# Products of ones on the tensor engine between the counts of a routing search, a fifth raw buffer, and a step that waits longer

## The chip, the cores and the metric

The kernel runs on one core of a Trainium2 chip, as one launch. The time is the device time of that core in microseconds (us), the median of three runs. TensorE (PE) multiplies, VectorE (DVE) and ScalarE (ACT) do elementwise work and move results out of PSUM, the matmul's output memory; GpSimd (POOL) issues gathers, and SyncE (SP) issues the other transfers.

## The reference

Three layers follow each other on 2304 tokens of 512 numbers. The second decides which tokens go where, and the change stands there.

```python
# 1. attention: 4 x 8 heads, 576 positions, window of 128, bias by distance
x = attention(q, k, v)                      # 2304 x 512
# 2. capacity-limited mixture: 8 experts, 288 tokens each
logits = x @ w_gate                         # 2304 x 8
for idx in argsort(-logits.flatten()):      # greedy, best logit first
    tok, e = idx // 8, idx % 8
    if assigned[tok] < 0 and counts[e] < 288:
        assigned[tok] = e; counts[e] += 1
for e in range(8):
    out[assigned == e] = relu(x[assigned == e] @ w1[e]) @ w2[e]   # 512 -> 1024 -> 512
# 3. weighted mixture: 4 experts on every token
for e in range(4):
    out2 += p[:, e:e+1] * (relu(out @ m2w1[e]) @ m2w2[e])
```

## The kernel before

Each matmul of 32-bit numbers is done as three: operands are split into an upper and a lower part (`wh`, `wl`; `xh`, `xl`), and `mm3` adds upper x upper, upper x lower and lower x upper (lines 791 to 793 are `hid_mm`'s and `mm3`'s three products).

Attention runs until about 157 us. Then come the eight groups of the second layer, one for each expert that becomes full, in the order in which they do. Group g begins with a search (`routing_steps`): six rounds, each of a `count` (PE: how many tokens wish each expert above each of n thresholds; two rounds with 18 products, line 559, four with 9, line 562), `enough` (DVE, tiles `odd` and `sat`), `any` (PE, tile `ns`) and `narrow` (DVE, tiles `pen`, `th`, `ge`). It closes with `who` (DVE, `r`), `many` (PE, `c`), `which` (DVE, `mk`), `totals` (PE, `tot`), `left` (DVE), `before` (PE, `pf`), `placed`, `tables` and `at` (DVE, `ob`), `numbers` (PE, `ls`, 18 products), `whole` (DVE, `idx`) and `gather` (POOL, `xg`). The next group's search starts with `wish` and `codes` (DVE, from `logits` to `oh`). A step depends on the one before, so PE and DVE take turns in it.

Once the rows are gathered, PE turns them (`rows`, tile `tp`), makes the 32 hidden steps `hid` (tile `hp_a`) and the 32 output steps `y` of the group, and then the first part of the third layer on these rows (`hp_f`, `po_f`). Each product of `hid` and `y` needs a piece of the expert's weights: 16 pieces for each group, loaded by SP into one of `NRAW` raw buffers (`raw_a`), copied to the upper part by ACT (`up`, `wh_a`) and subtracted by DVE (`low`, `wl_a`). Before them stand 12 pieces of the third layer's first expert (`raw_b`, `wl_b`). From about 625 us on PE does the rest of the third layer (`hp_b`, `po`).

The order of all steps from the search on is laid out beforehand by `arranged`: a list scheduler with a planned time for each step, which on each engine takes the open step of the lowest rank (search 1, weight pieces and `hid`/`y` 3). A step of rank 3 stands back if a step of lower rank opens within 0.4 of its planned time. Each engine then executes its steps in that order and waits by semaphores.

PSUM tiles come from pools; `ps_y` has two buffers:

```python
ps_y = ctx.enter_context(tc.tile_pool(name="ps_y", bufs=2, space=PSUM))
```

Of the kernel before, what the change touches and what calls it, by code (L numbers as in the profile page):

```python
# [9 lines left out]
F32 = mybir.dt.float32  # L10
# [9 lines left out]
P = 128  # L20
# [5 lines left out]
def fused_kernel(ctx: ExitStack, tc: tile.TileContext, q, k, v, w_gate, w1, w2, probs, m2w1, m2w2, out, dbg=None):  # L26
# [13 lines left out]
    NK = DM // P  # L40
    XC = DM + E2
    CB = 96
    NRAW = 4
    NB = CAP // CB
    HALF = F // 2
    KW = math.lcm(SEQ, P)
# [22 lines left out]
    def bc(ap, shape):  # L69
        return ap.broadcast_to(shape)  # L70
# [751 lines left out]
    def routing_steps(g):  # L822
        d = grp[g]
        prev = ("placed", g - 1) if g > 0 else None
        if g > 0:
            def wish():
                best_tiles(g)
                wishes(g, 0, NTL)
                if g < E - 1:
                    jl = rsm.tile([E, E], F32, tag="jl", name=f"jl_{g}")  # L830
                    V.tensor_tensor_reduce(jl, rem[:E, :], ident[:E, :E], 1.0, 0.0, ALU.mult, ALU.add, best["left"])
            step(("wish", g), DVE_, 3.0 if g < E - 1 else 1.4, wish, [("left", g - 1), ("at", 0, 1) if g == 1 else None], 1)
            step(("codes", g), DVE_, 0.5 if g < E - 1 else 0.1, lambda: wish_codes(g, 0, NTL), [("wish", g), prev], 1)
        else:
            def wish0():
                jl = rsm.tile([E, E], F32, tag="jl", name="jl_0")
                V.tensor_tensor_reduce(jl, rem[:E, :], ident[:E, :E], 1.0, 0.0, ALU.mult, ALU.add, best["left"])
            step(("codes", 0), DVE_, 0.1, wish0, [], 1)
        last = ("codes", g)
        if g < E - 1:  # L840
            for r in range(len(ROUNDS)):
                wide = ROUNDS[r][1] == 64
                now = {}

                def bind(i, g=g, r=r, now=now):
                    def run():
                        if not now:
                            now["f"] = ops_round(g, r)
                        now["f"][i]()
                    return run  # L850
                nx = r + 1 < len(ROUNDS)
                step(("count", g, r), PE_, 0.7 if wide else 0.45, bind(0), [last, ("keep", g - 2) if g > 1 and r == 0 else None], 1)
                step(("enough", g, r), DVE_, 0.28 if wide else 0.45, bind(1), [("count", g, r)], 1)
                step(("any", g, r), PE_, 0.2, bind(2), [("enough", g, r)], 1)
                step(("narrow", g, r), DVE_, (0.6 + (1.6 if ROUNDS[r + 1][1] == 64 else 0.95)) if nx else 0.5, bind(3), [("any", g, r)], 1)
                last = ("narrow", g, r)
        who, how_many, which, expert, totals, left_over, before, placed, tables, at_place, numbers, whole, gather = (
            (lambda i: lambda *a: closers(g)[i](*a))(i) for i in range(13)
        )
        if g < E - 1:  # L860
            step(("who", g), DVE_, 1.4, who, [last], 1)
            step(("many", g), PE_, 0.2, how_many, [("who", g)], 1)
            last = ("many", g)
        step(("which", g), DVE_, 0.95, which, [last] + ([prev, ("keep", g - 2)] if g == E - 1 else []), 1)
        step(("expert", g), SP_, 1.3, expert, [("which", g)], 1)
        step(("totals", g), PE_, 0.25, totals, [("which", g)], 1)
        step(("left", g), DVE_, 0.8, left_over, [("totals", g)], 1)
        step(("before", g), PE_, 0.3, before, [("left", g)], 1)
        step(("placed", g), DVE_, 0.55, placed, [("before", g)], 1)
        step(("tables", g), DVE_, 1.0, tables, [("placed", g)], 2 if g else 0)  # L870
        half = NTL // 2
        step(("at", g, 0), DVE_, 0.95, lambda: at_place(0, half), [("tables", g)], 2 if g else 0)
        step(("at", g, 1), DVE_, 0.95, lambda: at_place(half, NTL), [("at", g, 0)], 2 if g else 0)
        step(("numbers", g), PE_, 0.95, numbers, [("at", g, 1)], 1)
        step(("whole", g), DVE_, 0.2, whole, [("numbers", g)], 1)
        step(("gather", g), POOL_, 3.1, gather, [("whole", g), ("rows", g - 1, NK - 1) if g > 0 else None], 1)
# [8 lines left out]

    LAND = 4.5
    npieces = 0

    def pieces(n, job_of, known, free, names):
        nonlocal npieces  # L890
# [239 lines left out]
    def arranged():  # L1130

        order, ends, free, opened = [], {}, {}, {}
        waits = {n: len(t[2]) for n, t in tasks.items()}
        after = {n: [] for n in tasks}
        for n, t in tasks.items():
            for o, _ in t[2]:
                after[o].append(n)
        number = {n: i for i, n in enumerate(tasks)}

        def open_(n):  # L1140
            eng, _, needs, _, _ = tasks[n]
            at = 0.0
            for o, us in needs:
                lag = us if us is not None else (0.0 if tasks[o][0] == eng else 0.25)
                at = max(at, ends[o] + lag)
            opened.setdefault(eng, {})[n] = at

        for n, w in waits.items():
            if w == 0:
                open_(n)  # L1150
        while any(opened.values()):
            found = None
            for eng, names in opened.items():
                if not names:
                    continue
                now = max(free.get(eng, 0.0), min(names.values()))
                can = [n for n, at in names.items() if at <= now]

                def rank_of(n):
                    return 0.5 if eng == DVE_ and tasks[n][3] == 3 and now - names[n] > 1.5 and ("gather", 0) in ends else tasks[n][3]  # L1160
                n = min(can, key=lambda n: (rank_of(n), number[n]))
                us, rank = tasks[n][1], rank_of(n)

                soon = [o for o, at in names.items() if at < now + 0.4 * us and tasks[o][3] < min(rank, 2 if eng == "PE" else 3)]
                if rank >= 3 and soon:
                    n = min(soon, key=lambda o: names[o])
                start = max(now, names[n])
                if found is None or start < found[0]:
                    found = (start, n)
            start, n = found  # L1170
            eng, us, *_ = tasks[n]
            del opened[eng][n]
            free[eng] = ends[n] = start + us
            order.append((start, len(order), n))
            for o in after[n]:
                waits[o] -= 1
                if waits[o] == 0:
                    open_(o)
        assert len(order) == len(tasks)
        return sorted(order), ends  # L1180

    planned, ends = arranged()
# [87 lines left out]
```

## Time and profile before

| | us |
|---|---|
| median of three runs (1283.14 to 1286.18) | 1283.77 |
| profiled execution | 1285.34 |
| its span, first to last instruction | 1283.6 |
| PE busy in the span | 1227.5 |
| DVE busy | 635.5 |
| ACT busy | 404.7 |
| POOL busy | 216.7 |

The profile is of one execution. PE's busy time counts each product from its start to its modelled end, and products overlap, so starts of neighbours give their rate. PEclk is the granted clock of TensorE as a share of 2.4 GHz; the two levels that occur are 1.0 and 0.5 (1.2 GHz). In a timeline row, what stands in brackets is the engine's idle time before the row and what ended it.

### The profile page before, as it was taken

The numbers are of one execution on the slowest core, as the hardware profiler recorded it, in microseconds if no ns is written. First come the engines' busy times: TensorE is split into PE (matmuls) and PEld (weight loads), VectorE is DVE, ScalarE is ACT, GpSimd is POOL, SyncE is SP. The second block draws the span as 40 slices with busy tenths as digits, with TensorE's granted clock in tenths as the row PEclk, the third lists the DMA queues.
The fourth block names the chain that finished last, engine by engine and source line by source line (L and its number), as shares of the span: only waits on it lengthen the run. The fifth ranks groups of instructions, "written<-read, shape, count | busy, mean of one in ns | idle before, by whom it ended". The sixth has DMA issues, their size and how long they took to land.

```text
span 1283.6 us, 21264 instructions
## 1 busy us (share of the span) xinstructions
PE 1227.5 (96%) x8209; PEld 1110.7 (87%) x8209; DVE 635.5 (50%) x1828; ACT 404.7 (32%) x1041; POOL 216.7 (17%) x264
## 2 busy tenths in 40 slices
PE   7999828999999999999999999999999999999998
PEld 6998727888889899999988899899999998888896
DVE  6999888898768674443122233222222222222222
ACT  8998733333233343443211111111111111111110
POOL 8877501010000000000000111101101100100112
PEclk9999957899999999999999999999999999999999
DMA  9653144454444244564850011001000100000111
GB/s 182 149 142 76 51 132 135 157 107 121 117 147 136 78 161 110 169 132 111 313 203 1 23 44 33 33 1 34 25 9 17 33 17 17 17 1 1 41 42 65
DMA packets 125012, 108.58 MB, mean 85 GB/s; under 512 B 76272, under 2 KB 91632, under 8 KB 124912
## 3 DMA queue, kind: packets, MB, share of 16 engines
q1 hardware_dynamic: 121936, 97.76, 27.9%
q0 software_dynamic: 2976, 9.48, 2.2%
q8 instruction: 64, 1.05, 0.3%
q14 instruction: 36, 0.29, 0.1%
HBM read 83.53 MB, written 23.68 MB: 84 GB/s over the span
## 4 chain that ended last, share of the span: by engine, by line
PE 71%; DVE 9%; issue 5%; POOL 1%; DMA 1%; ACT 0%; POOLq 0%; SPq 0%; DVEq 0%
PE hp_b L791 8%; PE hp_b L793 8%; PE hp_b L792 8%; PE po L791 7%; PE po L793 7%; PE po L792 7%; PE hp_a L791 3%; PE hp_a L792 2%; PE hp_a L793 2%; PE po_f L791 2%; PE hp_f L791 2%; PE hp_f L793 2%; PE hp_f L792 2%; PE po_f L792 2%; PE po_f L793 2%
## 5 line engine op out<-in xcount | busy, mean ns | idle before, releaser
L800 ACT ACTIVATE hh_b<-hp_b 128x384 fp32r<-128x384 f32 x156 | 76.7, 492 | 535.8 <-PE hp_b L793 535.8
L803 DVE SCALAR_TENSOR_TENSOR hl_b<-hp_b,hh_b 128x384 fp32r<-128x384 f32 x156 | 87.0, 557 | 264.0 <-ACT hh_b L800 264.0
L793 PE MATMUL hp_b<-yTh,wl_b 128*128 128x384 f32 x624 | 209.5, 336 | 0.0
L791 PE MATMUL hp_b<-yTh,wh_b 128*128 128x384 f32 x624 | 209.5, 336 | 0.0
L792 PE MATMUL hp_b<-yTl,wh_b 128*128 128x384 f32 x624 | 209.4, 336 | 0.0
L1210 DVE SCALAR_TENSOR_TENSOR acc<-po,pp,acc 128x512 f32<-128x512 f32 x126 | 94.6, 751 | 219.0 <-PE po L793 219.0
L791 PE MATMUL po<-wh_b,hh_b 128*128 128x512 f32 x468 | 184.8, 395 | 0.0
L793 PE MATMUL po<-wh_b,hl_b 128*128 128x512 f32 x468 | 184.7, 395 | 0.0
L792 PE MATMUL po<-wl_b,hh_b 128*128 128x512 f32 x468 | 184.6, 395 | 0.0
L760 POOL TENSOR_TENSOR wl_b<-raw_b,wh_b 128x512 fp32r<-128x512 f32 x44 | 56.0, 1292 | 536.0 <-ACT wh_b L755 439.8
L791 PEld LDWEIGHTS hp_b<-yTh,wh_b 128*128 128x128 f32 x624 | 117.2, 188 | 1.8
L792 PEld LDWEIGHTS hp_b<-yTl,wh_b 128*128 128x128 f32 x624 | 117.2, 188 | 1.7
L793 PEld LDWEIGHTS hp_b<-yTh,wl_b 128*128 128x128 f32 x624 | 117.2, 188 | 0.0
L793 PEld LDWEIGHTS po<-wh_b,hl_b 128*128 128x128 f32 x468 | 87.7, 187 | 21.4
L792 PEld LDWEIGHTS po<-wl_b,hh_b 128*128 128x128 f32 x468 | 87.7, 187 | 19.5
L791 PEld LDWEIGHTS po<-wh_b,hh_b 128*128 128x128 f32 x468 | 87.7, 187 | 19.4
L760 DVE TENSOR_TENSOR wl_a<-raw_a,wh_a 128x512 fp32r<-128x512 f32 x128 | 84.0, 683 | 2.9 <-ACT wh_a L755 1.9
L721 POOL DMA_INDIRECT xg<-x_dram,idx x24 | 24.4, 1018 | 360.2 <-PE po_f L793 100.4
L791 PE MATMUL hp_a<-xh,wh_a 128*128 128x288 f32 x256 | 80.7, 315 | 0.0
L755 ACT CAST wh_a<-raw_a 128x512 fp32r<-128x512 f32 x128 | 73.6, 618 | 21.7 <-DMA raw_a<-in_moe_w_dram 21.6
L791 PE MATMUL y<-hh_a,wh_a 128*128 128x288 f32 x256 | 78.8, 308 | 0.0
L793 PE MATMUL y<-hh_a,wl_a 128*128 128x288 f32 x256 | 76.8, 300 | 1.7 <-DVE wl_a L760 1.7
(219 smaller groups left out, 2506.7 us busy)
## 6 DMA issues: line engine op xcount, KB each, us to landing
raw_a<-in_moe_w_dram SPq DMA_DIRECT2D x128, 256.0 KB, 3.2
raw_b<-in_moe_w_dram SPq DMA_DIRECT2D x64, 256.0 KB, 2.7
x_dram<-x SPq DMA_DIRECT2D x18, 258.0 KB, 2.6
y_dram<-yh SPq DMA_DIRECT2D x8, 576.0 KB, 3.1
y_dram<-yl SPq DMA_DIRECT2D x8, 576.0 KB, 4.6
yTh<-y_dram SPq DMA_DIRECT2D x6, 768.0 KB, 9.1
yTl<-y_dram SPq DMA_DIRECT2D x6, 768.0 KB, 10.5
acc<-part_dram SPq DMA_DIRECT2D x6, 768.0 KB, 11.3
```

Of the source, the lines that this page charges most:

```text
L721: G.indirect_dma_start(out=xg[:, j, :], out_offset=None, in_=x_dram[:, :], in_offset=bass.IndirectOffsetOnAxis(ap=d["idx"][:, j : j + 1], ...
L755: S.copy(res[n][0][0][:, a, b], raw)
L760: eng.tensor_tensor(lo[:, a, b], raw, hi[:, a, b].bitcast(F32), ALU.subtract)
L791: T.matmul(o, ah, bh, start=first, stop=False)
L792: T.matmul(o, ah, bl, start=False, stop=False)
L793: T.matmul(o, al, bh, start=False, stop=last)
L800: S.activation(h[0][:, f, :n], hp[:, :n], AF.Relu)
L803: V.scalar_tensor_tensor(h[1][:, f, :n], hp[:, :n], 0.0, h[0][:, f, :n].bitcast(F32), ALU.max, ALU.subtract)
L1210: V.scalar_tensor_tensor(accs[ch][:, i, :], po, pe, accs[ch][:, i, :], ALU.mult, ALU.add)
```

## The change

A new step `warm` multiplies a 128 x 128 matrix of ones by 256 columns of ones, into a tile of `ps_y` that nobody reads. 500 of them are offered to the planner on PE with a planned time of 0.115 us and rank 9, behind every other step; they stand back if a step of rank below 3 opens within 0.115 us. When the planner takes the first hidden step of group 0, those left over are dropped. `NRAW` becomes 5. The `wish` of group 1 waits for `whole` of group 0 in place of the last `at`. Until the first gather is planned, a weight piece stands back for a step that opens within 0.8 of its time.

```diff
-    NRAW = 4
+    NRAW = 5
...
-            step(("wish", g), DVE_, 3.0 if g < E - 1 else 1.4, wish, [("left", g - 1), ("at", 0, 1) if g == 1 else None], 1)
+            step(("wish", g), DVE_, 3.0 if g < E - 1 else 1.4, wish, [("left", g - 1), ("whole", 0) if g == 1 else None], 1)
...
+    def warm():
+        o = ps_y.tile([P, 512], F32, tag="y", name="warm")
+        T.matmul(o[:, :256], ones_bf, bc(ones_bf[:, None, :], [P, 2, P]), start=True, stop=True)
+
+    for i in range(500):
+        step(("warm", i), PE_, 0.115, warm, [("codes", 0)], 9)
...
-                soon = [o for o, at in names.items() if at < now + 0.4 * us and tasks[o][3] < min(rank, 2 if eng == "PE" else 3)]
+                near = 1.0 if rank == 9 else 0.4 if ("gather", 0) in ends else 0.8
+                soon = [o for o, at in names.items() if at < now + near * us and tasks[o][3] < min(rank, 2 if eng == "PE" and rank < 9 else 3)]
...
+            if n == ("hid", 0, 0, 0, 0):
+                for o in [o for o in opened[PE_] if o[0] == "warm"]:
+                    del opened[PE_][o]
...
-        assert len(order) == len(tasks)
+        assert all(n in ends or n[0] == "warm" for n in tasks)
```

PE, between the last two products of the first count and the product `ns` of the first round, as it stands before:

```order
L559 MATMUL cnt_0_3822<-ge_106,oh 8x64
L559 LDWEIGHTS oh
L559 MATMUL cnt_0_3822<-ge_106,oh 8x64
L578 LDWEIGHTS ones_bf
L578 MATMUL ns_0_3848<-sat_0_3821,ones_bf 128x64 [waits DVE_49]
L559 LDWEIGHTS oh
```

The same place now, from the last product of the count on; in brackets is the engine whose semaphore an instruction waits for:

```order
L559 MATMUL cnt_0_3822<-ge_106,oh 8x64
L893 LDWEIGHTS ones_bf
L893 MATMUL warm<-ones_bf 128x256
L893 LDWEIGHTS ones_bf
L893 MATMUL warm<-ones_bf 128x256
L893 LDWEIGHTS ones_bf
L893 MATMUL warm<-ones_bf 128x256 [waits PE_49]
L893 LDWEIGHTS ones_bf
L893 MATMUL warm<-ones_bf 128x256 [waits PE_49]
L893 LDWEIGHTS ones_bf
L893 MATMUL warm<-ones_bf 128x256 [waits PE_49]
L893 LDWEIGHTS ones_bf
```

Six `warm` stand between the count and `ns`; from the third on each waits for PE's own semaphore at the value that the `warm` two before it sets when it ends. Of all 304 that the planner placed, 302 wait so. They stand in runs of 6 (behind `cnt`), 23 (behind `ns`), 6, 17, then three times 8 and 17, then 8, 20 (ahead of `c`), 12 (ahead of `tot`), 11 (ahead of `pf`) and 34 (ahead of `ls`), which makes 212; behind `ls`, in the second group's search, 41, 6, 23, 6 and 12 ahead of the first `tp`; and 4 ahead of the first hidden product. The first `tp` stands behind the second group's second round; before, it stood behind the third.

DVE, behind `tables` of group 0 (`ob` is the last `at`), before:

```order
L694 TENSOR_TENSOR one_4097<-A_4090 128x54
L696 TENSOR_TENSOR R_4099<-one_4097,cp 128x108 [waits DVE_49]
L700 TENSOR_TENSOR ob_4101<-iotaB,bb_4095 128x864 x2
L117 TENSOR_TENSOR logits<-logits,capv 128x144
L118 TENSOR_REDUCE m_4106<-logits 128x18 [waits DVE_49]
```

and now:

```order
L694 TENSOR_TENSOR one_4467<-A_4460 128x54
L696 TENSOR_TENSOR R_4469<-one_4467,cp 128x108 [waits DVE_49]
L700 TENSOR_TENSOR ob_4471<-iotaB,bb_4465 128x864 x2
L716 TENSOR_REDUCE idx_4561<-ls_4532 96x3 [waits PE_49]
L117 TENSOR_TENSOR logits<-logits,capv 128x144
```

The `idx` that the gather waits for stands ahead of the second group's `wish` (which begins with `logits`); before, it stood behind it. On PE the order of counts, closing products, hidden and output products is otherwise the one that the planner's new times give; the second group's 16 weight pieces `wl_a` all stand on DVE ahead of that group's closing step `which`, where before the last three stood behind it.

## Rows read from the trace of the kernel before

**Rows 1.** Page: busy us by engine; granted clock in 40 slices, tenths.

```profile
PE 1227.5 (96%) x8209; PEld 1110.7 (87%) x8209; DVE 635.5 (50%) x1828; ACT 404.7 (32%) x1041; POOL 216.7 (17%) x264
...
PEclk9999957899999999999999999999999999999999
```

**Rows 2.** Windows: stretch, length, busy PE PEld DVE ACT POOL, clock, DMA, GB/s.

```profile
160.40:204.00 43.60, 14.26 (x151) 11.38 (x150) 38.26 (x123) 13.55 (x23) 4.45 (x3) 0.50 0.48 153
204.00:208.20 4.20, 4.20 (x19) 3.89 (x18) 2.76 (x11) 1.95 (x5) 0.00 (x0) 0.50 0.30 72
224.00:230.00 6.00, 3.11 (x31) 2.06 (x29) 5.62 (x24) 0.73 (x2) 0.00 (x0) 0.89 0.14 45
230.00:235.50 5.50, 5.50 (x27) 5.22 (x27) 4.22 (x9) 0.81 (x2) 0.00 (x0) 0.50 0.29 94
235.50:1240.00 1004.50, 1000.52 (x5998) 909.21 (x5996) 416.71 (x966) 237.29 (x508) 84.66 (x74) 1.00 0.26 77
```

**Rows 3.** Timeline of PE in the search: start, length, count, idle before.

```profile
157.17 0.63 PE L559 MATMUL cnt<-ge,oh 128*8 128x64 bf16 x16 [0.61 <-DVE lh L467]
158.78 0.22 PE L559 MATMUL cnt<-ge,oh 128*8 128x64 bf16 x2 [0.97 <-DVE oh L133]
159.36 0.18 PE L578 MATMUL ns<-sat,ones_bf 8*128 8x64 bf16 x1 [0.36 <-DVE sat L570]
161.18 1.30 PE L559 MATMUL cnt<-ge,oh 128*8 128x64 bf16 x18 [1.64 <-DVE ge L108]
...
169.65 0.80 PE L562 MATMUL cnt<-ge,oh 128*64 128x64 bf16 x9 [1.45 <-DVE ge L108]
171.11 0.20 PE L578 MATMUL ns<-sat,ones_bf 8*128 8x32 bf16 x1 [0.66 <-DVE sat L574]
...
187.40 1.85 PE L708 MATMUL ls<-R,ob 128*96 128x6 bf16 x18 [4.07 <-DVE ob L700]
...
201.10 1.70 PE L944 MATMUL tp<-ident,xg 96*128 96x96 f32 x9
...
203.98 0.59 PE L791 MATMUL hp_a<-xh,wh_a 128*128 128x288 f32 x1
204.37 0.44 PE L792 MATMUL hp_a<-xl,wh_a 128*128 128x288 f32 x1
204.61 0.44 PE L793 MATMUL hp_a<-xh,wl_a 128*128 128x288 f32 x1
```

**Rows 4.** Timeline of PE behind the first hidden product.

```profile
208.45 0.29 PE L793 MATMUL hp_a<-xh,wl_a 128*128 128x288 f32 x1
208.58 0.29 PE L791 MATMUL hp_a<-xh,wh_a 128*128 128x288 f32 x1
...
226.07 0.40 PE L793 MATMUL y<-hh_a,wl_a 128*128 128x288 f32 x1 [1.26 <-DVE wl_a L760]
227.64 0.69 PE L559 MATMUL cnt<-ge,oh 128*8 128x64 bf16 x18 [1.17 <-DVE oh L133]
...
229.24 0.61 PE L793 MATMUL y<-hh_a,wl_a 128*128 128x288 f32 x1 [0.46 <-DVE wl_a L760]
...
237.28 0.93 PE L708 MATMUL ls<-R,ob 128*96 128x6 bf16 x18
...
240.47 0.47 PE L562 MATMUL cnt<-ge,oh 128*64 128x64 bf16 x9
```

**Rows 5.** By tile: products' ns, least, median and most, from start to end.

```profile
L653 PE MATMUL tot<-ones_bf,mk x8: 231/231/291, 182.2 to 482.3; 128*36 128x128 bf16 x8
L791 PE MATMUL y<-hh_a,wh_a x45: 288/295/402, 236.0 to 300.0; 128*128 128x288 f32 x45
```

**Rows 6.** Timelines of DVE and POOL in the search: `sat`, `idx`, first gather.

```profile
159.04 0.27 DVE L570 TENSOR_SCALAR sat<-cnt,left 8x64 bf16<-8x64 f32 x1 [0.32 <-PE cnt L559]
...
191.22 0.15 DVE L716 TENSOR_REDUCE idx<-ls 96x3 int32<-96x6 f32 x1
...
191.67 1.17 POOL L721 DMA_INDIRECT xg<-x_dram,idx  x1 [37.96 <-DVE bm L131]
```

## Prediction

> **What bounds the kernel now.** I read the clock line and the TensorE line of the page first, then busy times by stretch, then the timelines of TensorE and VectorE from the first count on. TensorE has work in 96% of the span, and there is one long dip in the granted clock [rows 1]. The stretches [rows 2] say where. From 235.5 us to 1240 us TensorE is busy for 1000.5 of 1004.5 us at the full clock (2.4 GHz), so whatever starts that stream later ends the kernel later by as much. From 160.4 to 204 us it is busy for 14.3 of 43.6 us, at half clock (1.2 GHz): the first expert is being searched for, and products of 64 columns alternate with VectorE steps [rows 3]. The search ends for TensorE when the first expert's rows are turned (201.10 us) and the first hidden product starts (203.98 us). Behind it the clock stays at half until 208.2, and between 230 and 235.5 it is at half again, after three waits in the output products of 1.26, 1.17 and 0.46 us [rows 2, 4].
>
> **What the change puts on TensorE.** 304 products `warm` stand there before the first hidden product: 212 up to the products `ls` that number the rows (6, 23, 6, 17, then 8 and 17 in turn, 8, 20, 12, 11 and 34), 88 from there to the first `tp` (41, 6, 23, 6, 12) and 4 behind the last `tp`. The plan gives each 0.115 us. A stream without waits would come near that: 288 columns start every 0.13 us at full clock and every 0.24 us at half clock [rows 3, 4], so 256 columns every 0.12 us or 0.21 us.
>
> But 302 of the 304 wait for TensorE's own semaphore. `ps_y` has two buffers, so each `warm` waits until the one two before it has ended. The trace has no row in which TensorE waits for a product just issued; I build the price from two others. How long one takes from start to end: 0.231 us for 128 columns, 0.295 us for 288 [rows 5], so about 0.28 us for 256. How long a hand-over takes: the first count ends at 158.78 + 0.22 = 159.00 and `sat` starts at 159.04; `sat` ends at 159.31 and `ns` starts at 159.36 [rows 3, 6]; so 0.05 us. Two `warm` then take 0.28 + 0.05 = 0.33 us, each 0.165 us; as the first two of a run don't wait, I take 0.16 us on the mean. Bounds: 0.12 us if the wait never holds, 0.23 us if all ran at half clock (0.40 us from start to end, from the 0.44 us of 288 columns in [rows 3], plus 0.05, for two).
>
> At 0.16 us a run of `warm` is longer than the VectorE step beside which it stands, everywhere. Between `ns` and the next count VectorE now keeps TensorE idle for 1.64 us (wide round) and 1.45 us (narrow) [rows 3]; 23 and 17 `warm` take 3.7 and 2.7 us. Between a count and `ns` it is 0.36 and 0.66 us; 6 and 8 take 0.9 and 1.2 us. Ahead of `ls` it is 4.07 us; 34 take 5.5 us. The engine executes in order, so the count behind a run waits for it. TensorE's own stream then sets the length of the search.
>
> **The sum up to the first hidden product.** First count at 157.17, to 158.86 as now: 1.7 us. 300 `warm` x 0.16 = 48.0 us. At full clock three wide counts take 0.7 us each, four narrow ones 0.33 us each (0.47 us less the drain of the last), `ls` 0.9 us [rows 4]: 4.3 us. Twelve single products, 0.1 us each: 1.2 us. Together 55.2 us, so the first `tp` stands at 212.4 us against 201.10. From there 12 `tp` at half of now's 0.19 us, one count and 4 `warm` take 2.0 us (now 2.9 us): first hidden product at 214.4 us against 203.98, **10.4 us later**.
>
> **What comes back.** If the clock is at full when the hidden products start, the 4.2 us at half clock in 204.0 to 208.2 shrink by half: 2.1 us. With full clock in 230 to 235.5 too: 2.75 us. The three waits (2.9 us) I leave as they are. Weight pieces `wl_a` are nearer done when the hidden products start, and the new order has all 16 done before the second expert's closing steps; but its count rounds are one further behind and their products now stand between the hidden ones, so waits for `wl_a` turn into waits for `ge`, `r`, `mk` and `oh`. Bounds: 0 to all 2.9 us.
>
> Sum: 10.4 - 2.1 - 2.75 = **+5.6 us**. The profiled execution took 1285.34 us (span 1283.6 and 1.7 us around it), so it would take 1290.9 us; that run lies 1.6 us above the median of the runs shown, 1283.77, so the median becomes **1289.4 us**.
>
> **The parts I cost at nothing.** (a) `wish` of expert 1 behind `idx`. Now `ls` ends at 189.25, and `idx` waits behind that step until 191.22 [rows 3, 6]: 1.9 us for the gather. With the sum above the gather starts near 197.1 and has landed by 206.5 (9.43 us at most, 191.67 to 201.10 [rows 3, 6]), 6 us before TensorE gets to `tp`. Cover: 88 `warm`. Without it this part is worth those 1.9 us. (b) The wider look-ahead (0.8 of a step) before the first gather: VectorE takes one piece instead of two between `ge` and `odd`, which would be worth up to one piece; the 8 `warm` cover it. (c) The fifth raw buffer: loads run earlier, but in the search no piece is what TensorE waits for, and from 235.5 us on TensorE waits for 4.0 us in all.
>
> **A rule against my price.** The Trainium skill, "TensorE: Matmul & The Clock Gate", section "Back-to-back issue gap", gives about 109 ns from one such product to the next at full clock. The rows of 288 columns agree within 10 ns (133 against 122 ns), but none of them waits for its own engine. By it the sum would be that of the first rival.
>
> **Rivals.**
> 1. *The wait doesn't hold* (13%): 0.12 us each. 300 x 0.04 = 12 us less, of which VectorE takes back about 1 us ahead of `ls` and before `tp`: `tp` near 201.4, hidden products near 203.4, 0.6 us earlier than now. With 2.1 + 2.75 us back: 5.4 us faster, 1278.4 us. It decides below 0.14 us, where the search is 6 us shorter than in my sum. For it: the plan's own figure. Against it: the semaphore wait stands in the program.
> 2. *The clock falls among the products* (11%). Each pair leaves a pause, and the idle time around the first counts could drop the clock as it does now (half from 160.4 on [rows 2]). In a part at half clock a `warm` costs 0.07 us more; half of the 300 is 10 us, and the 2.1 us may not come back: near 1300 us. The same page of the Trainium skill ("A second HAM failure mode: psum-queue depth-cycling") reports a clock that swings where products cycle through PSUM banks with short pauses; no stretch of this trace shows such cycling. Against it: at half clock the same products stand nearly end to end, and the hidden products, end to end, brought the clock back at 208.2.
> 3. *The delay is taken up later* (14%). While TensorE is kept, VectorE gets ahead; then the three waits (2.9 us) go, and some of the 4.0 us after 235.5: 5.6 - 2.9 - 2 = +1 us, 1284.5 us, no difference that can be told. Against it: VectorE is in order, its pieces stand between steps that wait for TensorE.
> 4. *No effect* (2%): runs shorter than the steps beside them; 1284 us.
>
> **Chances and range.** About 0.3% (3.9 us) is what a measurement of this kernel tells from no change: 1279.9 and 1287.6. My case has 60%. Within it, 0.15 to 0.18 us for each is -3 to +6 us, and the waits give up to 2.9 us: 1283.5 to 1295.5 us. Some 8 of the 60 end below 1287.6. Slower: 52 + 11 = 63%. Same: 8 + 14 + 2 + 1 = 25%. Faster: 12%. The range leaves out the lower part of rival 1 and the upper part of rival 2: 1279 to 1298.
>
> **What the profile will show.** Right: `warm` starts in pairs, about 0.11 and 0.22 us apart in turn; 304 of them cover 48 us; every count of the search starts right behind a `warm` with no idle time whose releaser is VectorE; VectorE idles instead, waiting for `cnt` and `ns`; `ls` near 195.7, first `tp` near 212, first hidden product near 214, at full clock from its first row; no half clock around 230 to 245. Wrong: `warm` 0.12 us apart (rival 1), PEclk of 0.5 between 160 and 214 (rival 2), or a hidden product 10 us late but TensorE without idle time until the gap is made up (rival 3). The sum hangs most on the time of a pair: 0.01 us there is 1.5 us of it.

## The result, and the profile after

The changed kernel took 1297.35 us (median of four runs, 1295.53 to 1300.48) beside 1283.80 us for the kernel before on the same chip: 13.55 us slower, ratio 1.0104 with a 95% interval of 1.0092 to 1.0116. The forecast was 1289.4 us, 5.6 us slower. The direction and the range hold; the size is off by 8 us. The profiled execution is the slowest of the four (1300.48 us, span 1298.8), so its rows stand 3.1 us above the median.

The page of the changed kernel answers [rows 1]: TensorE's busy time and its clock in 40 slices.

```profile
PE 1268.9 (98%) x8513; PEld 1132.1 (87%) x8513; DVE 635.1 (49%) x1828; ACT 403.4 (31%) x1041; POOL 217.2 (17%) x264
...
PEclk9999999999999999999999999999999999999999
```

The long dip in the clock is gone (two of 3.5 and 3.4 us are left, too short to show in these slices), TensorE is busier by 41 us, and the kernel is slower: busy time that nobody needs. The windows answer [rows 2] (length, busy PE, PEld, DVE, ACT, POOL, clock, DMA, GB/s):

```profile
160.40:216.00 55.60, 55.34 (x438) 33.33 (x436) 38.55 (x123) 14.38 (x26) 3.52 (x3) 1.00 0.42 126
216.00:232.00 16.00, 12.95 (x107) 11.71 (x108) 10.87 (x33) 5.53 (x13) 0.00 (x0) 1.00 0.46 66
232.00:235.50 3.50, 3.50 (x16) 3.19 (x16) 3.17 (x12) 0.41 (x1) 0.00 (x0) 0.51 0.00 0
235.50:286.70 51.20, 46.23 (x373) 40.22 (x373) 43.15 (x148) 16.86 (x37) 3.99 (x3) 1.00 0.52 143
286.70:290.10 3.40, 3.40 (x25) 3.28 (x20) 2.72 (x10) 0.41 (x1) 0.00 (x0) 0.50 0.29 85
290.10:1240.00 949.90, 946.78 (x5611) 861.45 (x5610) 379.58 (x854) 220.01 (x471) 79.31 (x68) 1.00 0.23 74
```

TensorE's timeline in the search and at the first hidden product answers [rows 3, 4]:

```profile
157.18 0.63 PE L559 MATMUL cnt<-ge,oh 128*8 128x64 bf16 x16 [0.61 <-DVE lh L467]
...
158.94 1.04 PE L893 MATMUL warm<-ones_bf 128*128 128x256 bf16 x6
159.92 0.20 PE L578 MATMUL ns<-sat,ones_bf 8*128 8x64 bf16 x1
160.05 3.86 PE L893 MATMUL warm<-ones_bf 128*128 128x256 bf16 x23
163.84 0.69 PE L559 MATMUL cnt<-ge,oh 128*8 128x64 bf16 x18
...
191.44 5.59 PE L893 MATMUL warm<-ones_bf 128*128 128x256 bf16 x34
196.87 0.93 PE L708 MATMUL ls<-R,ob 128*96 128x6 bf16 x18
...
213.47 0.66 PE L953 MATMUL tp<-ident,xg 96*128 96x96 f32 x6
...
215.98 0.37 PE L791 MATMUL hp_a<-xh,wh_a 128*128 128x288 f32 x1 [0.26 <-DVE sat L574]
```

A run of 23 products lasts 3.86 us; the last takes 0.27 us from start to end, so 22 starts lie (3.86 - 0.27) / 22 = 0.163 us apart. The first count waits for `oh` as before; behind it no count waits for VectorE until the hidden products start. The first hidden product starts 12.0 us later than before [rows 3]; the first count stands where it stood, at 157.2 us. Up to here it is the forecast, with 1.6 us too little.

Behind it the forecast fails. Before, the first product of the third layer's remainder (`hp_b`) started at 625.0 us, 421.0 us behind the first hidden product; now it is 640.1, 424.1 us behind it. Of the delay nothing came back in this execution; 3.1 us were added. These are the windows of that stretch, before and then after, which show TensorE idle for 7.2 us (421.00 - 413.81) and 11.2 us. (The changed kernel's stretch also holds one round more of the second search, which stood ahead of the first hidden product before.)

```profile
204.00:625.00 421.00, 413.81 (x3087) 378.48 (x3086) 272.87 (x789) 150.26 (x334) 19.98 (x21) 0.99 0.48 133
```

```profile
216.00:640.10 424.10, 412.95 (x3095) 377.21 (x3095) 272.41 (x793) 148.13 (x332) 21.51 (x21) 0.99 0.45 132
```

Where the idle time comes from is read from the timelines of SyncE's queue (SPq), ScalarE, VectorE and TensorE of the changed kernel, put together in order of time:

```profile
214.89 0.43 SPq L970 DMA_DIRECT2D id_dram<-idx  x1
215.44 0.39 SPq L971 DMA_DIRECT2D p_dram<-xg  x1
217.10 4.92 SPq L747 DMA_DIRECT2D raw_a<-in_moe_w_dram  x3
227.51 0.62 ACT L755 CAST wh_a<-raw_a 128x512 fp32r<-128x512 f32 x1 [4.86 <-DMA raw_a<-in_moe_w_dram]
228.03 0.40 ACT L800 ACTIVATE hh_a<-hp_a 128x288 fp32r<-128x288 f32 x1
228.47 0.46 DVE L803 SCALAR_TENSOR_TENSOR hl_a<-hp_a,hh_a 128x288 fp32r<-128x288 f32 x1 [3.78 <-ACT hh_a L800]
230.12 0.76 DVE L108 TENSOR_TENSOR ge<-m,th 128x576 bf16<-128x576 f32 x1
230.94 0.47 PE L562 MATMUL cnt<-ge,oh 128*64 128x64 bf16 x9 [3.06 <-DVE ge L108]
```

Read it from the bottom: TensorE waits 3.06 us for `ge` of the second search; VectorE makes `ge` late because `hl_a`, ahead of it, waited 3.78 us for `hh_a`; ScalarE makes `hh_a` late because the cast ahead of it waited 4.86 us for a weight piece; and that piece was issued behind the two small writes of `keep` (token numbers and shares, `id_dram` and `p_dram`). The chain that ended last has two such pieces on it, one behind the writes of each of the first two groups:

```profile
217.10 10.39 DMA raw_a<-in_moe_w_dram
...
272.92 9.81 DMA raw_a<-in_moe_w_dram
```

The list of waits gives ScalarE's sum behind the first hidden product, before (from 204 us) and after (from 216 us), both to 640 us: total, times, longest.

```profile
ACT wh_a L755 <- DMA raw_a<-in_moe_w_dram: 4.2, 6, 1.1
```

```profile
ACT wh_a L755 <- DMA raw_a<-in_moe_w_dram: 15.4, 5, 7.4
```

Behind two of the TensorE waits (3.06 us ahead of 230.94, 2.78 us for `oh` ahead of 286.37) the clock is at half for 3.5 and 3.4 us, as the windows show.

### The profile page after: what moved, and what is told of

Read it like the earlier page. It is cut to its first block, busy times and chain, and to the rows that moved or that the text cites. A ratio compares the mean times of both kernels' runs of the same rounds, so it can differ in the third digit from the quotient of the medians.

```text
span 1298.8 us, 21872 instructions
## 1 busy us (share of the span) xinstructions
PE 1268.9 (98%) x8513; PEld 1132.1 (87%) x8513; DVE 635.1 (49%) x1828; ACT 403.4 (31%) x1041; POOL 217.2 (17%) x264
## 4 chain that ended last, share of the span: by engine, by line
PE 73%; DVE 6%; issue 4%; DMA 3%; POOL 1%; ACT 0%; POOLq 0%; SPq 0%; DVEq 0%
PE hp_b L793 8%; PE hp_b L791 8%; PE hp_b L792 8%; PE po L791 7%; PE po L793 7%; PE po L792 7%; PE warm L893 4%; DMA raw_a<-in_moe_w_dram 3%; PE hp_a L791 3%; PE hp_a L792 2%; PE hp_a L793 2%; PE y L791 2%; PE po_f L791 2%; PE y L793 2%; PE y L792 2%
## 5 line engine op out<-in xcount | busy, mean ns | idle before, releaser
L792 PE MATMUL hp_a<-xl,wh_a 128*128 128x288 f32 x256 | 76.7, 300 | 0.0
```

The lines of the kernel that those rows point to most:

```text
L792: T.matmul(o, ah, bl, start=False, stop=False)
```

## The experiments

Three theories were set against each other. **A**: a product that waits for TensorE's own semaphore costs 0.163 us, and the products make the loss. **B**: the other parts of the change (fifth buffer, waiting `wish`, wider look-ahead) put the weight pieces in an order that costs the later waits. **C**: the pieces are late because they follow the small writes of `keep`.

All results in one table. "Count" is the start of the search's first count, "first" the first hidden product; "then" the time from there to the first `hp_b`; "ScalarE" its wait for `raw_a` in that stretch; these four are of one profiled execution each, whose time stands under "profiled". The median is of 4 to 12 runs, the ratio against the kernel before on the same chip (1283.8 to 1285.0 us).

Three things have to be kept in mind with it. The attention ahead of the search is the same in all kernels, yet the first count stands between 155.4 and 157.3 us: what the search itself takes is "first" less "count". In before, e2, e6, e9, e13 and e14 one round more of the second search stands ahead of "first", and so not in "then". And a profiled execution can lie off its median: that of e1 is the slowest of its ten, 3.9 us above it.

| kernel | median us | ratio, 95% | profiled | count | first | then | ScalarE |
|---|---|---|---|---|---|---|---|
| before | 1283.8 |  | 1285.3 | 157.2 | 204.0 | 421.0 | 4.2 |
| changed | 1297.35 | 1.0104 (1.0092 to 1.0116) | 1300.5 | 157.2 | 216.0 | 424.1 | 15.4 |
| e1 no products | 1283.43 | 0.9986 (0.9977 to 0.9996) | 1287.3 | 157.3 | 201.7 | 425.2 | 16.7 |
| e2 products alone | 1299.12 | 1.0108 (1.0092 to 1.0125) | 1298.9 | 157.1 | 218.5 | 420.0 | 7.8 |
| e3 one tile | 1286.91 | 1.0012 (1.0000 to 1.0024) | 1289.2 | 156.1 | 201.7 | 427.1 | 18.0 |
| e4 planned 0.165 | 1286.17 | 1.0015 (1.0005 to 1.0026) | 1284.1 | 157.2 | 202.6 | 421.2 | 13.2 |
| e5 writes last | 1292.82 | 1.0070 (1.0057 to 1.0083) | 1291.1 | 155.7 | 214.5 | 416.2 | 5.8 |
| e6 five buffers alone | 1282.63 | 0.9983 (0.9975 to 0.9992) | 1281.9 | 157.2 | 204.1 | 417.4 | 6.2 |
| e7 one tile, writes last | 1279.86 | 0.9958 (0.9945 to 0.9971) | 1280.6 | 157.1 | 202.3 | 417.9 | 3.2 |
| e8 0.165, writes last | 1280.32 | 0.9963 (0.9950 to 0.9975) | 1281.1 | 157.2 | 202.7 | 418.0 | 2.5 |
| e9 before, writes last | 1284.39 | 0.9995 (0.9986 to 1.0003) | 1284.5 | 157.1 | 204.1 | 420.0 | 3.6 |
| e10 writes by ScalarE | 1296.70 | 1.0101 (1.0085 to 1.0117) | 1297.7 | 155.8 | 215.6 | 421.7 | 14.5 |
| e12 no products, writes last | 1278.03 | 0.9953 (0.9941 to 0.9966) | 1278.0 | 157.0 | 201.4 | 416.2 | 4.4 |
| e13 five buffers, writes last | 1279.36 | 0.9965 (0.9952 to 0.9979) | 1277.6 | 155.4 | 202.1 | 415.1 | 4.1 |
| e14 products alone, writes last | 1296.25 | 1.0095 (1.0079 to 1.0110) | 1296.0 | 155.9 | 217.0 | 418.6 | 8.2 |

### e1: the change without its products

```diff
-    for i in range(500):
+    for i in range(0):
         step(("warm", i), PE_, 0.115, warm, [("codes", 0)], 9)
```

> The change without its products: fifth raw buffer, waiting wish and wider look-ahead stay, 0 `warm`. Theory A (the products keep TensorE, and the rest of the change costs nothing): `ls` near 187, first hidden product at 201 to 205 us (before: 203.98), half clock again in the search, 1281 to 1286 us. Theory B (the order of weight pieces that comes with the other parts costs the 6.8 us that were lost behind the first output rows): ScalarE still waits for `raw_a` 10 us or more behind the search (before 4.2 us, changed kernel 15.4 us), TensorE waits behind `ge`, `sat` and `oh` of the third search, 1289 to 1293 us.

Measured 1283.43 us, 1.6 us under before. The loss is the products'. But ScalarE waits 16.7 us in the profiled execution (the slowest of ten), and TensorE stalls at the same place as in the changed kernel, so B's waits are there as well, paid for by a start that is 2.3 us earlier:

```profile
218.48 0.55 PE L562 MATMUL cnt<-ge,oh 128*64 128x64 bf16 x9 [3.44 <-DVE ge L108]
```

### e2: the products alone on the kernel before

```diff
-    NRAW = 5
+    NRAW = 4
...
-            step(("wish", g), DVE_, 3.0 if g < E - 1 else 1.4, wish, [("left", g - 1), ("whole", 0) if g == 1 else None], 1)
+            step(("wish", g), DVE_, 3.0 if g < E - 1 else 1.4, wish, [("left", g - 1), ("at", 0, 1) if g == 1 else None], 1)
...
-                near = 1.0 if rank == 9 else 0.4 if ("gather", 0) in ends else 0.8
+                near = 1.0 if rank == 9 else 0.4
```

> The products alone on the kernel before: four raw buffers, the old wish and look-ahead; 312 `warm`, 310 of them with a wait for TensorE's own semaphore. Theory A: each again 0.163 us, first hidden product 11 to 14 us later than before (215 to 218 us), 3 to 5 us given back at full clock, 1290 to 1296 us. Theory B: the first hidden product as late, but the later loss (ScalarE's waits of 4.9 and 7.4 us for `raw_a`, TensorE's behind `ge` and `oh`) is absent: near 1291 us, with less than 6 us of ScalarE's wait for `raw_a` behind the search; with 10 us or more of it the products themselves would cause that loss too, near 1297 us.

Measured 1299.12 us, above all that was expected: 14.1 us for the products alone. The first hidden product is 14.5 us late and 1.0 us comes back. Here too ScalarE waits for a piece behind the writes (4.6 us at its longest), and TensorE for 3.4 us behind it, at `mk`. The late piece is therefore no matter of the fifth buffer: B falls as the cause of the whole, though e1 shows that B's order of the pieces has such waits without any product.

### e3: all products into one PSUM tile

```diff
+    warm_in = []
+
     def warm():
-        o = ps_y.tile([P, 512], F32, tag="y", name="warm")
-        T.matmul(o[:, :256], ones_bf, bc(ones_bf[:, None, :], [P, 2, P]), start=True, stop=True)
+        if not warm_in:
+            warm_in.append(ps_y.tile([P, 512], F32, tag="y", name="warm"))
+        T.matmul(warm_in[0][:, :256], ones_bf, bc(ones_bf[:, None, :], [P, 2, P]), start=True, stop=True)
```

> The changed kernel with the same 304 `warm`, all into one PSUM tile that is taken once, so that none waits for TensorE's own semaphore. Theory A (the wait for the buffer sets 0.163 us): starts 0.11 us apart (the short distance of a pair now), so 304 x 0.053 = 16 us less on TensorE, of which VectorE's own steps take back a few: `ls` near 186, first hidden product 201 to 206 us, full clock through the search; 10 to 14 us less than the changed kernel, 1283 to 1288 us. Rival (the engine takes 0.16 us for such a product with its weight load whatever it waits for): starts 0.15 us or more apart, first hidden product near 216, 1295 to 1300 us.

Measured 1286.91 us, 11.8 us less than the changed kernel by the ratios (1.0012 against 1.0104 of 1284 us). The order on TensorE is the same; only the wait for its own semaphore is gone. Its timeline:

```profile
158.79 2.69 PE L896 MATMUL warm<-ones_bf 128*128 128x256 bf16 x23
161.41 0.69 PE L559 MATMUL cnt<-ge,oh 128*8 128x64 bf16 x18
...
201.67 0.37 PE L791 MATMUL hp_a<-xh,wh_a 128*128 128x288 f32 x1
```

The run of 23 takes 2.69 us, (2.69 - 0.27) / 22 = 0.110 us each: A holds. The first hidden product is 14.3 us earlier than in the changed kernel, 2.3 us earlier than before (1.0 us of either is the earlier start of this search), at full clock. Yet the kernel is no faster than before: from there on it takes 427.1 us in the profiled execution, and TensorE's list of waits in that stretch begins with the same three as in the changed kernel (3.1, 2.8 and 1.6 us there), one of them larger:

```profile
PE cnt L562 <- DVE ge L108: 5.7, 1, 5.7
PE cnt L559 <- DVE oh L133: 2.9, 1, 2.9
PE ns L578 <- DVE sat L574: 1.6, 2, 1.3
```

### e4: a planned time of 0.165 us

```diff
-        step(("warm", i), PE_, 0.115, warm, [("codes", 0)], 9)
+        step(("warm", i), PE_, 0.165, warm, [("codes", 0)], 9)
```

> The changed kernel with 0.165 us planned for a `warm` in place of 0.115: 208 are placed, 206 wait for TensorE's own semaphore. Theory A: each still takes 0.163 us, but 96 fewer are 15.6 us less on TensorE; runs are now about as long as VectorE's steps: first hidden product 202 to 207 us, full clock, 10 to 14 us less than the changed kernel, 1283 to 1288 us. Theory B (loss by order of the pieces, not by the products): the first hidden product is early, but ScalarE's waits for `raw_a` of 10 us or more come back, 1288 to 1293 us.

Measured 1286.17 us; 208 products, each as dear as in the changed kernel (16 of them in 2.68 us, 0.161 us each), and the search is as short as with one tile. So the loss in the search is the planner's: it filled 0.163 us steps into gaps by a figure of 0.115.

### e5 and e9: the small writes behind the group's last piece

```diff
-        step(("keep", g), SP_, 1.2, keep, [(("gather", g), 10.0), (("rows", g, NK - 1), 1.0)], 2)
+        step(("keep", g), SP_, 1.2, keep, [(("gather", g), 10.0), (("rows", g, NK - 1), 1.0), ("load", 2 * NFF + 16 * g + 15)], 2)
```

e5 is this edit on the changed kernel, e9 on the kernel before.

> The changed kernel, but the two small writes of a group (`id_dram`, `p_dram`) are issued behind the group's last weight piece, not ahead of its last two or three. Theory C (the pieces behind these writes land late: 10.4 us from issue to the cast that waits for it, 2.6 us elsewhere; ScalarE waits 4.9 and 7.4 us, and VectorE and TensorE behind it): ScalarE's wait for `raw_a` behind the search falls from 15.4 us to under 5 us, TensorE's waits of 3.06, 2.78 and 1.56 us in the second and third search fall to under 1 us each, no half clock at 232 and 287 us; the first hidden product stays at 216 us, the end is 6 to 9 us earlier than the changed kernel's: 1288 to 1292 us. Rival (the pieces are late because the fifth buffer lets loads run into each other, or because the engines' order is tight there anyway): the same waits remain, 1295 to 1298 us.

> The control: the kernel before, with the small writes behind the group's last weight piece. Theory C: before, no piece behind these writes is waited for longer than 1.1 us, so little is to be had: within 2 us of before. If it is 4 us or more faster, the late pieces were a loss of the kernel before as well, by another way than ScalarE's wait.

e5 measured 1292.82 us: by the ratios 4.4 us less than the changed kernel, a little short of what C expected. SyncE's queue in e5, and ScalarE's sum and TensorE's longest waits behind the first hidden product (at 214.5 us):

```profile
210.03 10.53 SPq L747 DMA_DIRECT2D raw_a<-in_moe_w_dram  x6
220.60 0.43 SPq L970 DMA_DIRECT2D id_dram<-idx  x1
```

```profile
ACT wh_a L755 <- DMA raw_a<-in_moe_w_dram: 5.8, 7, 1.8
...
PE tot L653 <- DVE mk L642: 1.9, 5, 0.4
PE ns L578 <- DVE sat L574: 1.7, 1, 1.7
```

The waits of 3 us for `ge` and `oh` are gone (0.7 us for `oh` is left), as is the half clock, and 4.8 us of the delay come back (416.2 us against 421.0). The wait of 1.7 us behind `sat` stays. TensorE's products stand in the same order in e5's trace and in the changed kernel's, so it isn't a new order of them that helps. e9 measured 1284.39 us, no change. Why the kernel before loses nothing by its small writes is seen in its own timelines of SyncE's queue and ScalarE:

```profile
204.57 0.39 SPq L962 DMA_DIRECT2D p_dram<-xg  x1
209.30 5.88 SPq L747 DMA_DIRECT2D raw_a<-in_moe_w_dram  x4
...
214.57 0.61 ACT L755 CAST wh_a<-raw_a 128x512 fp32r<-128x512 f32 x1
```

and in the time to landing of these four pieces:

```profile
DMA to landing us min/median/max: 2.8/3.7/5.0
```

The first of the four took the longest, 5.0 us, and landed at 214.3 us. The cast at 214.57 us is the one that uses it: it was just in time, by 0.3 us. Behind the writes of the second group, from 259.71 us on, a piece took 9.8 us to land in the kernel before too, but ScalarE had no cast of a weight piece between 264.00 and 279.37 us, and none waited.

### e6: the fifth buffer alone

```diff
-    NRAW = 4
+    NRAW = 5
```

> The kernel before with the fifth raw buffer alone. Theory C: with five buffers the last three pieces of the group are issued right behind the small writes, and ScalarE needs them while they are late: over 8 us of wait for `raw_a` behind the search (before 4.2 us), TensorE waits near 3 us more, half clock for 3.4 us: 2 to 5 us slower than before, with a wider spread between executions. Rival (the fifth buffer is free or helps, and the late pieces come with the new order of the wish and the look-ahead): within 1.5 us of before.

Measured 1282.63 us, 1.7 us faster; theory C had expected a loss and missed. With a fifth buffer two more pieces go out ahead of the writes, and ScalarE's longest wait for `raw_a` behind the first hidden product is 2.4 us, not near 5. The buffer is no cost in itself.

### e7 and e8: both causes taken away

e7 is e3 with the edit of e5, e8 is e4 with it.

> One PSUM tile for all products, and the small writes behind the group's last weight piece. If the two causes are apart and add up: first hidden product near 202 us as with one tile alone, full clock from its first row, none of the waits of 5.7, 2.9 and 1.3 us behind `ge`, `oh` and `sat` over 1 us: 7 to 10 us less than one tile alone (1286.91 us), 1277 to 1280 us, less than before. If the late pieces have another cause: 1284 to 1288 us.

> 0.165 us planned for a product (208 of them, still two buffers) and the small writes behind the group's last weight piece. If the price of a product and the late pieces are the two causes: as with one tile and late writes (1279.86 us): first hidden product near 202.6 us at full clock, ScalarE's wait for `raw_a` behind it under 6 us in place of 13.2, 5 us less than 0.165 alone (1286.17 us): 1279 to 1282 us. If the late pieces do not matter here: 1284 to 1288 us.

Measured 1279.86 and 1280.32 us, as expected: 4.5 and 3.9 us less than the kernel before by the medians, 0.42% and 0.37% by the ratios. From the changed kernel to e7 the ratios give 18.7 us, a little more than the 11.8 of one tile and the 4.4 of the late writes: two causes, each of which takes effect without the other.

### e10: the writes from another queue

```diff
-            nc.sync.dma_start(id_dram[gs, :].rearrange("(j i) o -> i (j o)", i=CB), grp[g]["idx"])
-            nc.sync.dma_start(p_dram[gs, :].rearrange("(j i) e -> i j e", i=CB), grp[g]["xg"][:, :, DM:])
-        step(("keep", g), SP_, 1.2, keep, [(("gather", g), 10.0), (("rows", g, NK - 1), 1.0)], 2)
+            nc.scalar.dma_start(id_dram[gs, :].rearrange("(j i) o -> i (j o)", i=CB), grp[g]["idx"])
+            nc.scalar.dma_start(p_dram[gs, :].rearrange("(j i) e -> i j e", i=CB), grp[g]["xg"][:, :, DM:])
+        step(("keep", g), ACT_, 1.2, keep, [(("gather", g), 10.0), (("rows", g, NK - 1), 1.0)], 2)
```

> The changed kernel, with the small writes at their old place in the program's order but issued by ScalarE, into its queue, not SyncE's. If a weight piece is late because it stands behind them in the same queue: ScalarE's wait for `raw_a` behind the search falls from 15.4 us to under 6 us and the time comes to 1290 to 1294 us, as with the writes issued last (1292.82 us). If the packets hold up the pieces from any queue: waits of over 10 us remain, 1295 to 1299 us.

Measured 1296.70 us, as the changed kernel. The first wait is a little shorter, 3.2 us; the second, ahead of 278.8 us, is 7.0. From ScalarE's timeline:

```profile
214.75 0.35 ACTq L970 DMA_DIRECT2D id_dram<-idx  x1
...
225.43 0.62 ACT L755 CAST wh_a<-raw_a 128x512 fp32r<-128x512 f32 x1 [3.16 <-DMA raw_a<-in_moe_w_dram]
```

So it isn't the place in SyncE's queue that makes a piece late. What the runs show is that ScalarE waits long for it in the changed kernel's order when the small writes are issued ahead of it, from either queue (e10), and not when they are issued behind it (e5).

### e12: no products, writes last

e1 with the edit of e5.

> No products, small writes last, the rest of the change as it is. What are the products worth where they cost the search nothing? The one-tile kernel with late writes has its first hidden product near 202.3 us at full clock; without products it was at 201.7 us, with half clock until 205.1 us, 3.4 us that cost 1.7 us. So the products would be worth about 1 us: this kernel at 1279.5 to 1282.5 us, with half clock until about 205 us. If they were worth the 4 us by which the half clock of the kernel before is longer (208.2 us against 204 us): 1283 to 1285 us.

Measured 1278.03 us, the fastest of all, 0.9953 of before (0.9941 to 0.9966). Its windows in the search, at the start of the hidden products and behind:

```profile
160.00:201.40 41.40, 13.46 (x140) 10.72 (x140) 36.44 (x117) 13.98 (x24) 3.52 (x3) 0.50 0.53 161
201.40:204.50 3.10, 3.10 (x14) 2.79 (x13) 2.93 (x11) 1.59 (x4) 0.00 (x0) 0.51 0.50 174
204.50:640.00 435.50, 430.43 (x3205) 394.11 (x3204) 274.96 (x795) 155.00 (x343) 26.97 (x25) 1.00 0.48 146
```

Half clock costs it 1.5 us behind the first hidden product, and that is all the products could save there. In the search itself a wide count is shorter at full clock (0.69 us against 1.30 [rows 3]), but the products take that back: from the first count to the first hidden product e7 needs 45.2 us and e12 44.4 us. Between e7 and e12 (0.9958 and 0.9953) no difference can be told: the products are worth nothing measurable even at 0.110 us each.

### e13 and e14: which part gains, and where products alone lose theirs

e13 is e6 with the edit of e5, e14 is e2 with it.

> The kernel before with the fifth buffer and the small writes last: the changed kernel without products, without the waiting wish and without the wider look-ahead. Without products but with those two it ran 1278.03 us. With five buffers alone 1282.63 us, of which ScalarE's wait of 2.4 us and three waits of TensorE between 219 and 228 us (2.3 us) stand behind a piece that is behind the writes. If buffer and late writes make the gain: 1278.5 to 1281 us, these waits gone, the first hidden product at 204 us. If the waiting wish and the look-ahead make it (they bring the first hidden product 2.3 us ahead): 1281 to 1284 us.

> The products alone on the kernel before (1299.12 us), with the small writes last. The first hidden product was 14.5 us late there, and 1.0 us came back, where the half clock that is gone should have given 4.85. If the piece behind the small writes ate the rest (ScalarE's wait of 4.6 us, TensorE's of 3.4 us for `mk`, half clock for 3.4 us behind it): these go, and it is 4 to 6 us faster than products alone: 1293 to 1295.5 us. If four buffers keep the pieces late anyway: 1297.5 to 1300 us.

e13 measured 1279.36 us, so the gain is the buffer's and the late writes' together; e9 and e6 show that one without the other is worth 0 and 1.7 us (the intervals of e6 and e13 overlap a little). The planner also orders TensorE's steps anew from before to e6, and a little from e6 to e13; that is not separated from the two. The first hidden product at 202.1 us is no part of the gain: the first count is 1.8 us earlier than in e6, and 46.7 us lie between them (e6 46.9). What the waiting `wish` and the look-ahead add (e12) lies within the intervals. e14 measured 1296.25 us, 12.3 us above before, where the products alone were 14.1 above: short of the 4 to 6 us expected, and the intervals overlap. The wait for `mk` of 3.4 us is gone, but the three waits of before stand in the output products again (1.26, 1.17 and 0.46 us), with half clock behind them, and ScalarE waits 6.0 us for the first piece behind the writes' new place. With four buffers it is therefore not shown that the late piece ate what should have come back.

## Why the prediction was right in direction and wrong in size

**The price of a product: right.** 0.163 us against 0.16, and in a run the starts lie about 0.11 and 0.22 us apart in turn, as forecast. It is the wait for the buffer that makes it: 0.110 us without (e3). The Trainium skill, "TensorE: Matmul & The Clock Gate", section "Back-to-back issue gap", has 262 cycles for 256 columns at full clock, which is an estimate of 109 ns. With its 0.110 us e3 agrees; the kernel with two buffers does not, since each product there waits for the one two before it.

**TensorE's stream sets the search: right, but too small.** The first hidden product came 12.0 us later, not 10.4. `ls` stood at 196.87 us, not 195.7: 300 times 0.003 us is 0.9 of it. This term was 1.6 us too small.

**2.1 us back at the first hidden products: right as far as it goes.** The clock is full from the first row on. Rival 2 falls: it stays full through all pairs. The Trainium skill, in the same page as above ("TensorE: Matmul & The Clock Gate"), section "A second HAM failure mode: psum-queue depth-cycling", tells of a kernel whose clock swung while its products cycled through PSUM banks; here the granted clock stayed at 1.00 from 160.4 to 216 us.

**2.75 us back between 230 and 235.5 us: wrong.** There were 3.5 us at half clock at 232 us and 3.4 us at 287, each behind a new wait of about 3 us: 6.9 us against 6.8 before. (Before, the products slow down between 228.5 and 229.2 us, not at 230, so the forecast of 2.75 us counted a little too few.)

**The failed step** is in "What comes back": the 2.75 us, and the three waits that it left "as they are", with 2.9 us less as the other bound. Nothing of the 2.75 us came, and TensorE's idle time behind the first hidden product did not stay, it grew by 4.0 us (11.2 against 7.2). What both rested on is said in part (c) of "The parts I cost at nothing": "The fifth raw buffer: loads run earlier, but in the search no piece is what TensorE waits for, and from 235.5 us on TensorE waits for 4.0 us in all." I took the rows of before as a sign that the pieces had room. They had not: the first piece behind the small writes had 0.3 us to spare. When the hidden products were moved against the writes, ScalarE came 7.2 us behind `p_dram` (222.65 against 215.44 us) and not 10.0 us (214.57 against 204.57), and its wait went through VectorE to TensorE. The buffer itself is not to blame: e2 has four, and loses as much.

In the sum of the profiled execution: 12.0 us late; 4.0 us more idle time behind it; 2.1 us back for the 4.1 us of half clock that are gone (6.9 against 4.2 + 6.8); about 0.9 us for the round of the second search that now stands between the hidden products, which the prediction saw and gave no price (an estimate: in before's rows at 213 to 215 us a count of nine holds them up by 0.6 us and `ns` by 0.3 us); and 0.4 us that I can't place. That is the 15.2 us by which the span is longer.

With the writes moved away (e5) as much comes back as the forecast said, 4.8 us against 4.85, though not term by term: all 11.0 us of half clock are gone, which is 5.5 us, TensorE is idle for 0.9 us less (6.3 against 7.2), and the extra round takes 0.9 us. What e5 does not mend is the first term. Its first hidden product is only 10.5 us later than before's, but that is the luck of an earlier start:

```profile
155.72 0.63 PE L559 MATMUL cnt<-ge,oh 128*8 128x64 bf16 x16 [0.61 <-DVE lh L467]
...
214.51 0.37 PE L791 MATMUL hp_a<-xh,wh_a 128*128 128x288 f32 x1 [0.26 <-DVE sat L574]
```

From the first count to the first hidden product it needs 58.8 us, as the changed kernel does (before 46.8), so there too the products make it 12.0 us later. The median of e5 is 8.5 us above before, where the forecast was 5.6.

Of the 8.0 us by which the forecast fell short (5.6 against 13.55), e5 shows 4.4 as the late pieces', the first term has 1.6 in the profiled execution, and 2.0 stay open; the round without a price may be 0.9 of these.

**Rival 1** did not come, but e3 is its case: first hidden product at 201.7 us (forecast 203.4; its search began 1.0 us earlier), and no gain of 5.4 us, because of the late pieces; with these out of the way (e7) the gain is 4.5 us. **Rival 3** was the opposite of what happened: VectorE did not use the time to get ahead, it waited for ScalarE. **Parts (a) and (b)** start the hidden products some 2 us earlier where no product covers them (44.4 us behind the first count in e1, 46.8 before), in part because one round less stands ahead of them, and show in no time that can be told from noise (e12 against e13).

## What to carry to other kernels

Work that only fills time and has to take a buffer in turn runs at the pace of its own completion, not at its issue rate (here 0.163 us against 0.110): give it one buffer, or plan it with the pace that is measured, and ask first what the better clock can give back (here 1.5 us behind the search). Before costing a shift at nothing, look for transfers that were just in time: a piece with 0.3 us to spare was the sign, and the late pieces cost 4.4 us (e5), more than the clock could give. Small scattered writes belong behind the loads that someone is waiting for; with five buffers the median fell each time (e5, e7, e8, e12, e13), with four it did not (e9), or by no more than the intervals (e14). And before two profiles are compared, measure each from a step that is the same in both: e5's 10.5 us were 12.0.

## What the runs showed of the hardware

Two small writes go with slow loads around them, from either of two queues (e10). In the changed kernel, from 214.8 to 228 us, this is the DMA view (packets, bytes; queue, packets, MB, share of the 16 engines' time):

```profile
DMA packets 1351, 1.29 MB, mean 98 GB/s; under 512 B 723, under 2 KB 723, under 8 KB 1351
...
q1 hardware_dynamic: 1351, 1.29, 61.3%
...
id_dram<-idx SPq DMA_DIRECT2D x1, 1.1 KB
p_dram<-xg SPq DMA_DIRECT2D x1, 4.5 KB
```

Of 1351 packets 723 are under 512 bytes, the engines are busy for 61% of the time and move 98 GB/s, where in the search they moved 126 GB/s at 42%. A piece of 256 KB took 10.4 us from its issue to the cast that waited for it, and 2.5 us at the least from issue to landing elsewhere in this kernel:

```profile
DMA to landing us min/median/max: 2.5/3.2/9.7
```

In e5 a load behind the writes is slow as well: a piece issued at 271.99 us, behind those of the second group (from 267.69 us on), took 11.4 us to land. But ScalarE's longest wait for any piece there is 1.8 us.

One wait of TensorE of about 3 us was followed by about 3.4 us at half clock (twice in the changed kernel), a wait of 1.7 us (for `sat`) by none in e5 and by as much in e7. What decides between these last two the runs do not tell.
